# Attention heads paired for all four 64x64 tiles of the array, a state update in column halves, and a state without zero blocks

## The chip, the cores and the metric

The kernel runs on one core of a Trainium2 chip (trn2). Times are device microseconds of one execution. The time before is 762.54 us (median of six executions, 761.15 to 762.91). When the prediction was made three of these were known, with a median of 762.65.

## The reference, cut to what matters

Attention with a decaying state (batch 4, 8 heads, 768 steps, head size 64), followed by a two-layer block on 3072 tokens (512 to 2048 to 512, float32 results):

```python
for t in range(S):
    state = gamma[None, :, None, None] * state + np.einsum('bhd,bhe->bhde', k[:, :, t], v[:, :, t])
    y[:, :, t] = scale * np.einsum('bhd,bhde->bhe', q[:, :, t], state)
...
h = x @ w_in
g = h * erf(np.maximum(h, 0.0) + np.log1p(np.exp(-np.abs(h))))
return g @ w_out
```

## The kernel before

The sequence is cut into 24 chunks of 128 steps (four sequences of six chunks; c is the position in the sequence). A chunk goes through these steps: T transposes queries and keys, S makes the scores (64-row tiles), M masks them on VectorE, O makes the outputs, U makes the state's increment, A adds it to the state. These steps are strewn between the products of the two-layer block, which TensorE does with a seven-product (Strassen-like) scheme after the first 512 tokens. Chunks 0 to 3 come first. Chunks 4 to 7 lie beside the first 512 tokens. Chunks 8 to 23 lie in the long stretch from 163 us.

```python
def load(j):
    ...
    for x, src in ((KQ[j][:, 0], k), (KQ[j][:, 1], q), (V[j], v)):
        nc.sync.dma_start(x, src[b, :, c * C : (c + 1) * C, :].rearrange("h p d -> p h d"))
...
state = const.tile([P, HP, P], F32, name="state")      # a pair of heads: two 64x64 blocks, the rest zeros
nc.gpsimd.memset(state, 0.0)
...
def ret_out(j):
    ...
    p = ret_psum()
    if c:
        for hp in range(HP):
            nc.tensor.matmul(
                p[:, hp, :], state[:, hp, :], QT[j][:, hp, :],
                start=(hp == 0), stop=False, skip_group_check=True,
            )
    for hp in range(HP):
        for s in range(2):
            nc.tensor.matmul(
                p[s * D : (s + 1) * D, hp, :], V[j][:, 2 * hp + s, :], AM[j][:, s, hp, :],
                start=(not c and hp == 0), stop=True, skip_group_check=True,
            )
    nc.scalar.copy(XC[m][:, :, i * C : (i + 1) * C], p)

def ret_state(j):
    ...
        for hp in range(HP):
            nc.tensor.matmul(
                p[:, hp, :],
                KQ[j][:, 0, 2 * hp : 2 * hp + 2, :].rearrange("p h d -> p (h d)"),
                V[j][:, 2 * hp : 2 * hp + 2, :].rearrange("p h d -> p (h d)"),
                start=True, stop=True,
            )

def ret_add(j):
    for s in range(2):
        own = slice(s * D, (s + 1) * D)
        ... # state[own, :, own] += SU[j][own, :, own], or a copy at c == 0
```

The weights arrive as float64 and are converted on VectorE in small steps, which `pace(n)` deals out beside the other work. The last of them are the sums for the split products.

Of the kernel before, what the change touches and what calls it, by code (L numbers as in the profile page):

```python
# [12 lines left out]
F32 = mybir.dt.float32  # L13
# [3 lines left out]
ALU = mybir.AluOpType  # L17
PSUM = bass.MemoryType.PSUM

P = 128  # L20
C = 128
TCH = 512
FG = 4
SCH = 256
CV = 2



IN = {"11": 0, "12": 1, "21": 2, "22": 3, "S3": 2, "S1": 4, "S2": 5, "S4": 6}
# [12 lines left out]
def kernel(  # L42
# [13 lines left out]
    nc = tc.nc  # L56
    B, H, S, D = q.shape
    d_model, d_ff = w_in.shape
    HP = H // 2
    NC = S // C  # L60
    NJ = B * NC
    n_k = d_model // P
    n_ft = d_ff // P
# [2 lines left out]
    N = FG * TCH  # L66
    DH = d_model // 2
    assert D == 64 and d_model == H * D and n_k == HP == 4 and S % C == 0 and NJ % JPC == 0
    assert n_ft == 4 * FG and SCH == 2 * C and TCH == 2 * SCH

    const = ctx.enter_context(tc.tile_pool(name="const", bufs=1))
    loads = ctx.enter_context(tc.tile_pool(name="loads", bufs=3))
# [8 lines left out]
    KQ, V = {}, {}  # L81

    def load(j):
        b, c = divmod(j, NC)
        KQ[j] = loads.tile([P, 2, H, D], F32, name="kq")
        V[j] = loads.tile([P, H, D], F32, name="v")
        for x, src in ((KQ[j][:, 0], k), (KQ[j][:, 1], q), (V[j], v)):
            nc.sync.dma_start(x, src[b, :, c * C : (c + 1) * C, :].rearrange("h p d -> p h d"))

    kq_s = const.tile([P, NC, 2, H], F32, name="kq_s")  # L90
    d_s = const.tile([P, 2, HP], F32, name="d_s")

    w_in_sb = const.tile([P, 2, 7, 2, FG * P], F32, name="w_in_sb")
# [27 lines left out]
    place = [n % 4 if n < n_p - 4 else (n - n_p + 4) % 3 for n in range(n_p)]  # L121

    def load_piece(n):
        which, i = pieces[n]
        w = raws[place[n]]
        if which == "in":
            nc.sync.dma_start(
                w.rearrange("p (g f) -> p g f", g=n_k),
                w_in[:, i * 2 * P : (i + 1) * 2 * P].rearrange("(g p) f -> p g f", p=P),
            )  # L130
        else:
            for d in range(2):
                nc.sync.dma_start(
                    w.rearrange("p (d f c) -> p d f c", d=2, f=2)[:, d],
                    w_out[i * 2 * P : (i + 1) * 2 * P, d * DH : (d + 1) * DH].rearrange(
                        "(f p) c -> p f c", p=P
                    ),
                )
# [99 lines left out]
    def pace(n):  # L238

        nonlocal room  # L240
        room += n
        while room >= 1:
            next(weight_steps, None)
            room -= 1
# [5 lines left out]
            room -= 1  # L250

    load_piece(0)
    nc.scalar.dma_start(kq_s[:, 0, 0], decay_k)
    for s in range(2):
        nc.scalar.dma_start(d_s[:, s], decay_s[s * D : s * D + 1, :].to_broadcast([P, HP]))
    load(0)
    load_piece(1)
    load(1)
    load_piece(2)
    load(2)  # L260
    load_piece(3)

# [6 lines left out]
        out=causal, in_=causal, compare_op=ALU.is_ge, fill=0.0,  # L269
        base=0, pattern=[[1, C]], channel_multiplier=-1,  # L270
    )

    state = const.tile([P, HP, P], F32, name="state")
    nc.gpsimd.memset(state, 0.0)


    unscale = 1.0 / math.sqrt(D)
# [1 line left out]
    def query_scale(c):  # L279
        nc.vector.reciprocal(kq_s[:, c, 1], kq_s[:, c, 0])  # L280
        nc.vector.tensor_scalar(kq_s[:, c, 1], kq_s[:, c, 1], unscale, None, op0=ALU.mult)

    query_scale(0)

    def other_scales():
        back = const.tile([P, 2, HP], F32, name="back")
        nc.vector.reciprocal(back, d_s)
        for c in range(1, NC):
            by_head = [kq_s[:, i, 0].rearrange("p (h s) -> p s h", s=2) for i in (c, c - 1)]
            nc.gpsimd.tensor_tensor(by_head[0], by_head[1], back, op=ALU.mult)  # L290
        query_scale(slice(1, NC))


    QT, KT, SC, AM, XC, SU = {}, {}, {}, {}, {}, {}
# [4 lines left out]
    def ret_psum():  # L299

        pool = next(psum_turn) if early else ps_r
        return pool.tile([P, HP, C], F32, name="hp" if pool is ps_h else "r")
# [14 lines left out]
    def ret_transpose(j):  # L317
        assert j in scaled
        for i, (name, store) in enumerate((("k", KT), ("q", QT))):
            p = ret_psum()  # L320
            for hp in range(HP):
                nc.tensor.transpose(  # L322
                    p[:, hp, :],
                    KQ[j][:, i, 2 * hp : 2 * hp + 2, :].rearrange("p h d -> p (h d)"),
                    ident,
                )
            store[j] = ret.tile([P, HP, C], F32, name=name + "T")
            nc.scalar.copy(store[j], p)
        pace(1)
# [22 lines left out]
    def ret_out(j):  # L352
        c = j % NC
        m, i = divmod(j, JPC)
        if i == 0:
            XC[m] = ret.tile([P, HP, TCH], F32, name="xT")
        p = ret_psum()


        if c:  # L360
            for hp in range(HP):
                nc.tensor.matmul(  # L362
                    p[:, hp, :], state[:, hp, :], QT[j][:, hp, :],
                    start=(hp == 0), stop=False, skip_group_check=True,
                )
        for hp in range(HP):
            for s in range(2):
                nc.tensor.matmul(  # L368
                    p[s * D : (s + 1) * D, hp, :], V[j][:, 2 * hp + s, :], AM[j][:, s, hp, :],
                    start=(not c and hp == 0), stop=True, skip_group_check=True,  # L370
                )
        nc.scalar.copy(XC[m][:, :, i * C : (i + 1) * C], p)  # L372
        pace(1.7)

    def ret_state(j):
        c = j % NC
        if c < NC - 1:
            p = SU[j] = ret_psum()
            for hp in range(HP):
                nc.tensor.matmul(  # L380
                    p[:, hp, :],
                    KQ[j][:, 0, 2 * hp : 2 * hp + 2, :].rearrange("p h d -> p (h d)"),
                    V[j][:, 2 * hp : 2 * hp + 2, :].rearrange("p h d -> p (h d)"),
                    start=True,
                    stop=True,
                )
            pace(1)
        if j + 3 < NJ:
            load(j + 3)

    def ret_add(j):
        if j not in SU:
            return
        for s in range(2):
            own = slice(s * D, (s + 1) * D)
            if j % NC:
                nc.vector.tensor_tensor(
                    state[own, :, own], state[own, :, own], SU[j][own, :, own], op=ALU.add
                )
            else:  # L400
                nc.vector.tensor_copy(state[own, :, own], SU[j][own, :, own])
        pace(-0.8)


    HS, E, O = {}, {}, {}
# [76 lines left out]
    def chunk_of(g):  # L482
        return TCH // SCH + (g - G0) // 2
# [100 lines left out]
    def put_part(m, step):  # L584
# [26 lines left out]

    K_, T, S_, M, O_, U, A = (
        ret_scale, ret_transpose, ret_scores, ret_mask, ret_out, ret_state, ret_add
    )


    for f, *args in (
        (pace, 3), (K_, 0), (T, 0), (pace, 3.1), (S_, 0), (M, 0), (other_scales,), (K_, 1),
        (O_, 0), (T, 1), (U, 0), (pace, 1.5), (A, 0), (S_, 1), (M, 1), (K_, 2),
        (O_, 1), (T, 2), (U, 1), (pace, 1.5), (A, 1), (S_, 2), (M, 2), (K_, 3),  # L620
        (O_, 2), (T, 3), (U, 2), (pace, 0.5), (A, 2), (S_, 3), (pace, 0.5), (M, 3), (K_, 4),
        (O_, 3), (U, 3),
    ):
        f(*args)
# [29 lines left out]
    j = 2 * JPC  # L654
# [51 lines left out]
    g, m = NG - 1, chunk_of(NG - 1)  # L706
# [47 lines left out]
```

## Time and profile before

| | before |
|---|---|
| time, median of six | 762.54 us |
| TensorE busy | 731.1 us, 96% |
| 0 to 53 us | VectorE 41.6 of 53 us busy, DMA engines 0.92 to 0.99 |

The table by stage and its reading stand in the prediction.

```profile
PE hp L513 <- issue: 3.7, 1, 3.7
```

The columns are the waiter, what ended the wait, us in total, how often, and the longest. On the profile page below, "issue" is time in which the profile shows no cause.

### The profile page before, as it was taken

The numbers are of one execution on the slowest core, as the hardware profiler recorded it, in microseconds if no ns is written. First come the engines' busy times: TensorE is split into PE (matmuls) and PEld (weight loads), VectorE is DVE, ScalarE is ACT, GpSimd is POOL, SyncE is SP. The second block draws the span as 40 slices with busy tenths as digits, with TensorE's granted clock in tenths as the row PEclk, the third lists the DMA queues.
The fourth block names the chain that finished last, engine by engine and source line by source line (L and its number), as shares of the span: only waits on it lengthen the run. The fifth ranks groups of instructions, "written<-read, shape, count | busy, mean of one in ns | idle before, by whom it ended". The sixth has DMA issues, their size and how long they took to land.

```text
span 760.7 us, 11046 instructions
## 1 busy us (share of the span) xinstructions
PE 731.1 (96%) x4896; PEld 622.6 (82%) x4896; DVE 361.4 (48%) x482; ACT 272.4 (36%) x295; POOL 31.7 (4%) x29
## 2 busy tenths in 40 slices
PE   3889999989999999999999999999999999999996
PEld 2755445448699999999999999999999999999995
DVE  5897899994324334333253153163163152153323
ACT  1334636231533423414424424424234144324430
POOL 1000001000010110010010110100000000000000
PEclk9999999998999999999999999999999999999999
DMA  9977544102120120220220220220200000000000
GB/s 230 273 182 186 153 141 123 56 0 42 56 42 9 35 70 2 41 70 2 42 71 1 42 70 1 42 62 9 43 29 1 1 28 1 1 28 1 1 28 28
DMA packets 87391, 42.66 MB, mean 56 GB/s; under 512 B 76080, under 2 KB 76080, under 8 KB 87344
## 3 DMA queue, kind: packets, MB, share of 16 engines
q1 hardware_dynamic: 86912, 41.95, 21.4%
q8 instruction: 38, 0.62, 0.4%
q14 instruction: 9, 0.07, 0.0%
q10 hardware_dynamic: 432, 0.01, 0.0%
HBM read 35.66 MB, written 6.29 MB: 55 GB/s over the span
## 4 chain that ended last, share of the span: by engine, by line
PE 90%; DVE 5%; ACT 3%; issue 2%; DMA 1%; DVEq 0%; ACTq 0%
PE hp L513 33%; PE o L570 30%; PE o L456 7%; PE hp L443 6%; PE r L335 3%; PE r L368 3%; PE r L322 2%; PE r L362 2%; PE r L380 2%; DMA w_out_sb<-in_moe_w_in_dram 1%; ACT e L412 1%; DVE am L347 1%; DVE kq L313 1%; ACT e L413 1%; ACT L412 1%
## 5 line engine op out<-in xcount | busy, mean ns | idle before, releaser
L513 PE MATMUL hp<-xs,w_in_sb 128*128 128x128 f32 x1280 | 160.6, 280 | 3.9 <-issue 3.7
L513 PEld LDWEIGHTS hp<-xs,w_in_sb 128*128 128x128 f32 x1280 | 152.0, 193 | 10.8 <-issue 7.1
L570 PE MATMUL o<-w_out_sb,h 128*128 128x256 f32 x640 | 141.6, 379 | 0.0
L432 DVE TENSOR_TENSOR e<-h,e 128x1024 f32<-128x1024 f32 x44 | 51.9, 1221 | 182.7 <-ACT e L413 182.7
L570 PEld LDWEIGHTS o<-w_out_sb,h 128*128 128x128 f32 x640 | 121.6, 190 | 16.5
L513 PE MATMUL hp<-xT,w_in_sb 128*128 128x128 f32 x960 | 113.7, 275 | 0.0
L513 PEld LDWEIGHTS hp<-xT,w_in_sb 128*128 128x128 f32 x960 | 111.9, 192 | 1.9 <-issue 1.0
L570 PE MATMUL o<-w_out_sb,e 128*128 128x256 f32 x480 | 110.3, 379 | 0.9 <-DVE e L432 0.9
L570 PEld LDWEIGHTS o<-w_out_sb,e 128*128 128x128 f32 x480 | 88.2, 190 | 11.7 <-DVE e L432 1.3
L412 ACT ACT_TABLE_LOAD x24 | 30.8, 1283 | 91.4 <-PE o L570 89.4
L443 PE MATMUL hp<-xT,w_in_sb 128*128 128x512 f32 x128 | 58.9, 608 | 0.0
L538 DVE TENSOR_TENSOR h<-h,hp 128x512 f32<-128x512 f32 x20 | 13.7, 687 | 83.3 <-PE hp L513 83.3
L533 DVE TENSOR_TENSOR h<-h,hp 128x512 f32<-128x512 f32 x20 | 13.8, 688 | 80.7 <-ACT h L531 80.7
L313 POOL TENSOR_TENSOR kq<-kq,kq_s 128x1024 f32<-128x1024 f32 x15 | 29.1, 1940 | 498.3 <-DMA kq<-in_q_dram 476.8
L443 PEld LDWEIGHTS hp<-xT,w_in_sb 128*128 128x128 f32 x128 | 24.0, 194 | 27.0 <-issue 26.7
L372 ACT COPY xT<-r 128x512 f32<-128x512 f32 x24 | 14.0, 585 | 88.9 <-PE r L368 88.9
L412 ACT ACTIVATE e<-h 128x2048 f32<-128x2048 f32 x22 | 42.0, 1911 | 0.2
L413 ACT ACTIVATE e<-e 128x2048 f32<-128x2048 f32 x22 | 42.0, 1910 | 0.2
L347 DVE TENSOR_TENSOR am<-r,causal 128x512 f32<-128x512 f32 x44 | 28.5, 684 | 21.4 <-PE r L335 20.8
L322 PE MATMUL r<-ident,kq 128*128 128x128 f32 x176 | 24.8, 284 | 14.0 <-DVE kq L313 10.8
L536 ACT COPY h<-hp 128x512 f32<-128x512 f32 x20 | 11.7, 585 | 71.9 <-PE hp L513 71.9
L322 PEld LDWEIGHTS r<-ident,kq 128*128 128x128 f32 x176 | 21.0, 147 | 15.9 <-issue 12.1
(84 smaller groups left out, 694.1 us busy)
## 6 DMA issues: line engine op xcount, KB each, us to landing
w_out_sb<-in_moe_w_out_dram SPq DMA_DIRECT2D x14, 512.0 KB, 5.1
kq<-in_k_dram SPq DMA_DIRECT2D x24, 256.0 KB, 3.5
kq<-in_q_dram SPq DMA_DIRECT2D x24, 256.0 KB, 4.2
v<-in_v_dram SPq DMA_DIRECT2D x24, 256.0 KB, 4.5
w_in_sb<-in_moe_w_in_dram SPq DMA_DIRECT2D x6, 1024.0 KB, 5.5
out_dram<-r SPq DMA_DIRECT2D x24, 256.0 KB, 2.3
w_out_sb<-in_moe_w_in_dram SPq DMA_DIRECT2D x2, 1024.0 KB, 6.9
w_in_sb<-in_moe_w_out_dram SPq DMA_DIRECT2D x2, 512.0 KB, 3.9
```

The source lines that it names most:

```text
L313: engine.tensor_tensor(KQ[j], KQ[j], by, op=ALU.mult)
L322: nc.tensor.transpose(p[:, hp, :], KQ[j][:, i, 2 * hp : 2 * hp + 2, :].rearrange("p h d -> p (h d)"), ident,)
L335: nc.tensor.matmul(pp[s][:, hp, :], KT[j][s * D : (s + 1) * D, hp, :], QT[j][s * D : (s + 1) * D, hp, :], start=True, stop=True,)
L347: nc.vector.tensor_tensor(AM[j][:, s], SC[j][s], causal[:, None, :].to_broadcast([P, HP, C]), op=ALU.mult)
L368: nc.tensor.matmul(p[s * D : (s + 1) * D, hp, :], V[j][:, 2 * hp + s, :], AM[j][:, s, hp, :], start=(not c and hp == 0), stop=True, skip_g ...
L412: nc.scalar.activation(E[g], HS[g], AF.Softplus)
L413: nc.scalar.activation(E[g], E[g], AF.Erf)
L432: nc.vector.tensor_tensor(E[g][:, half], HS[g][:, half], E[g][:, half], op=ALU.mult)
L443: nc.tensor.matmul(p, w_in_of(ft, kk), XC[0][:, kk, :], start=(kk == 0), stop=(kk == n_k - 1))
L456: nc.tensor.matmul(O[0][tt].rearrange("p (d c) -> p d c", d=2), E[g][:, u * TCH + tt * P : u * TCH + (tt + 1) * P], w_out_of(ft), start=(f ...
L513: nc.tensor.matmul(bank[:, u, :], w_in_sb[:, s, IN[a], kk, u * P : (u + 1) * P], XS[m][b][:, kk, :], start=(p in (1, 2, 5) and u == 0 and ...
L570: nc.tensor.matmul(O[m][i][:, half, :], G[g][a][:, u * P : (u + 1) * P], w_out_sb[:, s, OUT[b], u, :], start=i not in started, stop=(s == ...
```

## The change

The intent is to do the two products that waste half of the array at half the work. The state loses its zero blocks. Each head's query-state product takes a 64x64 tile, and heads are paired so that successive products fall on all four. The state update makes only the diagonal blocks, two at a time in the halves of the columns. For this the heads of k and q are loaded in the order 0, 3, 1, 2, 4, 7, 5, 6, so that the two heads of a pair lie side by side for the transposes. This splits their transfers.

```diff
+PAIRS = ((0, 3), (1, 2), (4, 7), (5, 6))
+MOVES = ((0, 0), (3, 1), (1, 2), (2, 3))
 def load(j):
-        for x, src in ((KQ[j][:, 0], k), (KQ[j][:, 1], q), (V[j], v)):
-            nc.sync.dma_start(x, src[b, :, c * C : (c + 1) * C, :].rearrange("h p d -> p h d"))
+        for i, src in enumerate((k, q)):
+            for of, to in MOVES:
+                nc.sync.dma_start(
+                    KQ[j][:, i].rearrange("p (a b) d -> p a b d", a=2)[:, :, to],
+                    src[b, :, now, :].rearrange("(a b) p d -> p a b d", a=2)[:, :, of],
+                )
+        nc.sync.dma_start(V[j], v[b, :, now, :].rearrange("h p d -> p h d"))
 ... (the decay factors are put into the same order by eight tiny copies on VectorE)
-    state = const.tile([P, HP, P], F32, name="state")
-    nc.gpsimd.memset(state, 0.0)
+    state = const.tile([P, HP, D], F32, name="state")
 def ret_out(j):
-        p = ret_psum()
+        pp = [ret_psum() for _ in range(2)]
+        def place(h, r):
+            return pp[r][h % 2 * D : (h % 2 + 1) * D, h // 4, :]
         if c:
-            for hp in range(HP):
-                nc.tensor.matmul(p[:, hp, :], state[:, hp, :], QT[j][:, hp, :], ...)
+            for u, pair in enumerate(PAIRS):
+                for r, h in enumerate(pair):
+                    own = slice(r * D, (r + 1) * D)
+                    nc.tensor.matmul(place(h, r), state[own, u, :], QT[j][own, u, :], ...)
 ... (the value products go to the same places)
-        nc.scalar.copy(XC[m][:, :, i * C : (i + 1) * C], p)
-        pace(1.7)
+        for r in range(2):
+            nc.scalar.copy(XC[m][:, r::2, i * C : (i + 1) * C], pp[r][:, :2, :])
+        pace(1.5)
 def ret_state(j):
+            for u, pair in enumerate(PAIRS):
+                for r, h in enumerate(pair):
+                    nc.tensor.matmul(
+                        p[r * D : (r + 1) * D, u, :D], KQ[j][:, 0, 2 * u + r, :], V[j][:, h, :],
+                        start=True, stop=True,
+                    )
 def ret_add(j):
+        new = SU[j][:, :, :D]        # one instruction on 128 partitions instead of two on 64
-        pace(-0.8)
+        pace(-0.4)
```

More of the change, by code (lines that the diff above doesn't have):

```diff
@@ L68 @@
     assert D == 64 and d_model == H * D and n_k == HP == 4 and S % C == 0 and NJ % JPC == 0
-    assert n_ft == 4 * FG and SCH == 2 * C and TCH == 2 * SCH
+    assert H == 8 and n_ft == 4 * FG and SCH == 2 * C and TCH == 2 * SCH
     const = ctx.enter_context(tc.tile_pool(name="const", bufs=1))
@@ L86, in load @@
         V[j] = loads.tile([P, H, D], F32, name="v")
-        for x, src in ((KQ[j][:, 0], k), (KQ[j][:, 1], q), (V[j], v)):
-            nc.sync.dma_start(x, src[b, :, c * C : (c + 1) * C, :].rearrange("h p d -> p h d"))
+        now = slice(c * C, (c + 1) * C)
+        for i, src in enumerate((k, q)):
[5 more added lines that the diff above has]
+        nc.sync.dma_start(V[j], v[b, :, now, :].rearrange("h p d -> p h d"))
     kq_s = const.tile([P, NC, 2, H], F32, name="kq_s")
+    d_k = const.tile([P, H], F32, name="d_k")
     d_s = const.tile([P, 2, HP], F32, name="d_s")
@@ L252 @@
     load_piece(0)
-    nc.scalar.dma_start(kq_s[:, 0, 0], decay_k)
+    nc.scalar.dma_start(d_k, decay_k)
     for s in range(2):
@@ L281, in query_scale, with in_pairs @@
         nc.vector.tensor_scalar(kq_s[:, c, 1], kq_s[:, c, 1], unscale, None, op0=ALU.mult)
+    def in_pairs(to, of):
+        for a, b in MOVES:
+            nc.vector.tensor_copy(
+                to.rearrange("p (a b) -> p a b", a=2)[:, :, b],
+                of.rearrange("p (a b) -> p a b", a=2)[:, :, a],
+            )
+    in_pairs(kq_s[:, 0, 0], d_k)
     query_scale(0)
     def other_scales():
-        back = const.tile([P, 2, HP], F32, name="back")
-        nc.vector.reciprocal(back, d_s)
+        back, by = (const.tile([P, H], F32, name=name) for name in ("back", "by"))
+        nc.vector.reciprocal(back, d_s.rearrange("p s h -> p h s"))
+        in_pairs(by, back)
         for c in range(1, NC):
-            by_head = [kq_s[:, i, 0].rearrange("p (h s) -> p s h", s=2) for i in (c, c - 1)]
-            nc.gpsimd.tensor_tensor(by_head[0], by_head[1], back, op=ALU.mult)
+            nc.gpsimd.tensor_tensor(kq_s[:, c, 0], kq_s[:, c - 1, 0], by, op=ALU.mult)
         query_scale(slice(1, NC))
@@ L320, in ret_transpose @@
             p = ret_psum()
-            for hp in range(HP):
+            for u in range(HP):
                 nc.tensor.transpose(
-                    p[:, hp, :],
-                    KQ[j][:, i, 2 * hp : 2 * hp + 2, :].rearrange("p h d -> p (h d)"),
+                    p[:, u, :],
+                    KQ[j][:, i, 2 * u : 2 * u + 2, :].rearrange("p h d -> p (h d)"),
                     ident,
@@ L356, in ret_out @@
             XC[m] = ret.tile([P, HP, TCH], F32, name="xT")
-        p = ret_psum()
+        pp = [ret_psum() for _ in range(2)]
+        def place(h, r):
+            return pp[r][h % 2 * D : (h % 2 + 1) * D, h // 4, :]
         if c:
-            for hp in range(HP):
-                nc.tensor.matmul(
-                    p[:, hp, :], state[:, hp, :], QT[j][:, hp, :],
-                    start=(hp == 0), stop=False, skip_group_check=True,
-                )
-        for hp in range(HP):
-            for s in range(2):
-                nc.tensor.matmul(
-                    p[s * D : (s + 1) * D, hp, :], V[j][:, 2 * hp + s, :], AM[j][:, s, hp, :],
-                    start=(not c and hp == 0), stop=True, skip_group_check=True,
-                )
-        nc.scalar.copy(XC[m][:, :, i * C : (i + 1) * C], p)
-        pace(1.7)
+            for u, pair in enumerate(PAIRS):
+                for r, h in enumerate(pair):
+                    own = slice(r * D, (r + 1) * D)
+                    nc.tensor.matmul(
+                        place(h, r), state[own, u, :], QT[j][own, u, :],
+                        start=(h < 4), stop=False, skip_group_check=True,
+                    )
+        for h in range(H):
+            u, r = next((u, pair.index(h)) for u, pair in enumerate(PAIRS) if h in pair)
+            nc.tensor.matmul(
+                place(h, r), V[j][:, h, :], AM[j][:, r, u, :],
+                start=(not c and h < 4), stop=True, skip_group_check=True,
+            )
+        for r in range(2):
+            nc.scalar.copy(XC[m][:, r::2, i * C : (i + 1) * C], pp[r][:, :2, :])
+        pace(1.5)
     def ret_state(j):
@@ L378, in ret_state @@
             p = SU[j] = ret_psum()
-            for hp in range(HP):
-                nc.tensor.matmul(
-                    p[:, hp, :],
-                    KQ[j][:, 0, 2 * hp : 2 * hp + 2, :].rearrange("p h d -> p (h d)"),
-                    V[j][:, 2 * hp : 2 * hp + 2, :].rearrange("p h d -> p (h d)"),
-                    start=True,
-                    stop=True,
-                )
+            for u, pair in enumerate(PAIRS):
+                for r, h in enumerate(pair):
+                    nc.tensor.matmul(
+                        p[r * D : (r + 1) * D, u, :D], KQ[j][:, 0, 2 * u + r, :], V[j][:, h, :],
+                        start=True, stop=True,
+                    )
             pace(1)
@@ L393, in ret_add @@
             return
-        for s in range(2):
-            own = slice(s * D, (s + 1) * D)
-            if j % NC:
-                nc.vector.tensor_tensor(
-                    state[own, :, own], state[own, :, own], SU[j][own, :, own], op=ALU.add
-                )
-            else:
-                nc.vector.tensor_copy(state[own, :, own], SU[j][own, :, own])
-        pace(-0.8)
+        new = SU[j][:, :, :D]
+        if j % NC:
+            nc.vector.tensor_tensor(state, state, new, op=ALU.add)
+        else:
+            nc.vector.tensor_copy(state, new)
+        pace(-0.4)
     HS, E, O = {}, {}, {}
```

## The prediction

> **What bounds the kernel now.** I read four views in this order: the busy summary, the busy table by stretch, the matmul timeline of one chunk, and the chain of work that ended last. First the summary:
>
> ```profile
> PE 731.1 (96%) x4896; PEld 622.6 (82%) x4896; DVE 361.4 (48%) x482; ACT 272.4 (36%) x295; POOL 31.7 (4%) x29
> ```
>
> TensorE is busy for 96% of the span. That average hides two regimes, so I cut the span by stage:
>
> ```profile
> core 0: us, PE busy (x) PEld busy (x) DVE busy (x) ACT busy (x) POOL busy (x), PEclk, DMA share, GB/s
> 20.00:53.00 33.00, 28.21 (x216) 21.38 (x216) 30.16 (x38) 10.35 (x16) 0.00 (x0) 1.00 0.99 247
> 53.00:84.00 31.00, 29.23 (x146) 16.91 (x148) 24.90 (x29) 15.08 (x18) 0.00 (x0) 0.94 0.56 153
> 84.00:163.00 79.00, 79.00 (x248) 37.89 (x247) 76.97 (x74) 36.96 (x35) 4.38 (x2) 1.00 0.35 100
> 163.00:662.00 499.00, 495.31 (x3663) 456.04 (x3662) 183.69 (x280) 172.91 (x192) 24.72 (x13) 0.99 0.13 31
> ```
>
> From 163 us on, TensorE alone is the bound, and 16 of the 24 chunks of attention (numbers 8 to 23) run there. Before 53 us VectorE (30.2 of 33) and the DMA engines (share 0.99) are both nearly full, and TensorE is the follower. What a TensorE saving is worth is therefore read in the long stretch. One chunk of it, matmuls only:
>
> ```profile
> 441.00 1.04 PE L322 MATMUL r<-ident,kq 128*128 128x128 f32 x8
> 441.88 1.95 PE L513 MATMUL hp<-xs,w_in_sb 128*128 128x128 f32 x16
> 443.76 1.16 PE L335 MATMUL r<-qT,kT 64*128 64x128 f32 x16
> 444.85 2.05 PE L513 MATMUL hp<-xs,w_in_sb 128*128 128x128 f32 x16
> 446.74 1.06 PE L362 MATMUL r<-qT,state 128*128 128x128 f32 x8
> 447.73 1.09 PE L368 MATMUL r<-am,v 128*64 128x128 f32 x16
> ```
>
> The first column is the start. Differences of starts are what a block costs, because ends are modelled and overlap the next block. Each float32 product of the program is two records, so x8 is four products. L322 takes 441.88 - 441.00 = 0.88 for 8 records. In longer runs the rate is 3.57 us for 32 records, 0.1116 each. I call that one step.
>
> The two half-size blocks are the lesson. L335 (row halves) and L368 (column halves) have 16 records each, but last 1.09 and 1.02, not 16 x 0.1116 = 1.79. Two tiles run side by side, so each block is 8 steps = 0.893 plus 0.20 or 0.13. The extra is the price of changing the array's shape. L513 before L335 lasts 1.88 where 16 steps are 1.786, so 0.094 is lost at the change. L513 after L335 lasts 1.89, so 0.10 is lost at its beginning. L362 ahead of L368 lasts 0.99 where 8 steps are 0.893, again 0.094 at the change.
>
> So a change of shape costs 0.094 us to drain plus the first weight load, which is not hidden: about 0.10 us for 128 columns and about 0.045 for 64 (1.02 - 0.893 - 0.094 = 0.04). Weight loads support the ratio:
>
> ```profile
> L335 PEld LDWEIGHTS r<-qT,kT 64*128 64x128 f32 x352 | 25.1, 196 | 7.4 <-ACT qT L328 2.6 <-issue 2.5
> L368 PEld LDWEIGHTS r<-am,v 128*64 128x64 f32 x384 | 22.0, 140 | 6.9 <-DVE am L347 3.8 <-issue 0.8
> ```
>
> Half the columns save 56 ns, so a 64-column load occupies some 0.05 us.
>
> The chain of work that ended last puts what the change touches at 2.0% (L362) and 1.9% (L380) of the span:
>
> ```profile
> by line: PE hp L513 33.4%; PE o L570 30.0%; PE o L456 7.2%; PE hp L443 5.7%; PE r L335 3.2%; PE r L368 3.2%; PE r L322 2.4%; PE r L362 2.0%; PE r L380 1.9%; issue 1.6%; DMA w_out_sb<-in_moe_w_in_dram 0.8%; ACT e L412 0.8%; DVE am L347 0.6%;
> ```
>
> That is 30 us in all. Halving both at no cost would give 15 us, 2.0% of 762.65. This caps what TensorE can yield before the changes of shape are paid.
>
> **What the Trainium skill says.** "TensorEngine Tiling (Array Packing)", Key Properties, says that changing the tiling mode drains TensorE while changing only the tile does not. The trace agrees: 0.094 us at each change. "TensorE: Matmul & The Clock Gate", Part 3, says that a pack of tiles takes about one matmul and 4 ns per further tile, sixteen tiles included. For two tiles the trace agrees (16 records in about 8 steps); no run here has shown four. The same page, Part 1, gives a floor of about 25 ns between starts of matmuls. With four tiles the wanted spacing is 0.1116/4 = 28 ns, and with two tiles of 64 columns it is 30 ns. Both are barely above that floor, and the densest block in this trace has 56 ns. "DMA: Bandwidth & Descriptors", Rules for kernel authors, warns that transfers under 64 KB are mostly overhead. The loads of k and q go from 256 KB to exactly 64 KB each.
>
> **The change, part by part.**
>
> 1. *Query times state.* Four products with a 128x128 stationary operand, half of it zeros, become eight of 64x64 that can fill all four quadrants. 16 records in groups of four are 4 steps = 0.446 instead of 0.893: minus 0.447 us per chunk that has a state.
>
> 2. *State update.* Four 128x128 products, half of whose output is thrown away, become eight with 64 stationary columns and 64 moving columns, two side by side: 8 steps of a shorter kind. From 128, 256 and 512 moving columns (0.1116, 0.216, 0.429 us between starts) a column costs 0.00081 us, so 64 columns take 0.1116 - 0.052 = 0.060 us (estimate), just longer than the 0.05 us weight load beneath it. 8 x 0.060 = 0.48 instead of 0.893: minus 0.413 us.
>
> 3. *Changes of shape.* Query-state was of full shape like its neighbour; now its entry costs 0.094 + 0.045 = 0.139 more. Its exit to the value product was a change already. The state update stood between full-shape work; now it costs 0.139 to enter and 0.194 to leave. In sum plus 0.472 us per chunk, more than half of what parts 1 and 2 give.
>
> Chunks 8 to 23 hold 11 of positions 1 to 4 in their sequence (both parts): -0.447 - 0.413 + 0.472 = -0.388 each. Three stand at position 5 (no update): -0.447 + 0.139 = -0.308. Two stand at position 0 (no query-state): -0.413 + 0.333 = -0.080. The sum is 4.27 + 0.92 + 0.16 = 5.4 us, on the path because TensorE there never waits.
>
> Chunks 4 to 7 run at 59 to 122 us, mostly TensorE-bound. In chunk 4 the state update directly follows the value product in the same 128x64 shape, so it saves more, about 0.9; one score block also waits 0.6 us there for the state addition, which becomes shorter. With 0.3, 0.1 and 0.4 for the other three: about 2 us.
>
> 4. *VectorE.* The state addition was two instructions of about 0.42 us on 64 partitions; it becomes one of 128x256, and 128x256 float32 instructions of the same engine also take 0.42. Three such pairs lie on the early chain (30.83, 36.9, 42.11 us), and the copy at 23.80: about 1.5 us gained if VectorE holds there. Eight tiny copies come in for the head order: four while VectorE waits for the first weights anyway, four ahead of the scales, which chunk 1 waits for: 4 x 0.17 (the 128x8 instruction takes 171 ns) = about 0.6 us lost.
>
> 5. *ScalarE.* One eviction of 128x512 (0.585) becomes two of 128x256 (0.378 each), +0.17 us. The next user of those banks comes 16 records, 1.8 us, later: hidden.
>
> 6. *Loads.* Three transfers per chunk become nine, the same bytes and the same 256-byte rows. An issue occupies SyncE's queue for 0.37 us at least, so the query tile of chunk 0 is fully issued some 2 us later, but the 1 MB weight piece ahead of it keeps the engines busy until 6.7 us, and VectorE comes to it at 9.4 only. I allow +0.5 to +1 us before 53 us and nothing later, where loads run three chunks ahead.
>
> 7. *Order of conversion steps.* The pacing numbers shift by +0.2 step per chunk: within noise.
>
> Sum: -5.4 - 2.0 - 1.5 + 0.6 + 0.7 = -7.6 us, so 755.0 us.
>
> **Rivals.**
>
> *Four tiles don't run four at once.* If only two quadrants stream together, query-state takes 8 steps as before and the changes of shape remain: 18 chunk positions x 0.447 = 8 us come back and the time is about 763. For it: no block in this trace runs four tiles. Against: row halves and column halves each overlap nearly perfectly, and each row half writes its own bank.
>
> *The state update is bound by issue or weight loads, not by 64 columns.* If a pair still takes a full step of 0.11, the gain of 0.413 vanishes for 20 chunks and 0.333 is paid: about 762. For it: 4 instructions every 60 ns is twice the densest rate seen. Against: the weight load alone takes 0.05.
>
> *The early stretch gets worse.* Before 53 us the DMA engines are 99% busy; if 48 more transfers each cost them something, 1 to 3 us are added, and the saving of VectorE is lost: about 757 to 758.
>
> *A new wait for the masks.* Query-state now writes two banks, those of the scores, so it needs both masks. Where the second mask ends 446.41 and query-state starts 446.74, there is 0.33 us to spare, 0.33 to 0.50 in all later chunks: no wait expected.
>
> **Range and chances.** The middle case is 755.0. If all overlaps and the early part goes well, 752. If one of the first two rivals holds, 761 to 763. I hold each of those two at 15 to 20%, so the upper end gets more room: 751.5 to 761.5. The 2% marks are 747.4 and 777.9. The first is almost the cap of free halving, which the changes of shape forbid; the second would need several us of new waits.
>
> **What would show each step.** In the timeline after: starts of the query-state block and of the value block about 0.58 us apart (4 steps, 0.045, 0.094; 1.02 or more refutes four at once); the state update block about 0.62 (8 x 0.060 + 0.045 + 0.094); the block ahead of each longer by 0.094. The long stretch from the first split product to the last should be 5 to 6 us shorter. If chunk spacing there shrinks by less than 0.2 us per chunk, the tile arithmetic is wrong; if it shrinks by 0.39 and the total still doesn't, the early stretch is at fault.

## More of the kernel before

The long stretch, one group of products after the other:

```python
for g in range(G0, NG):
    if first:
        x_sums(g)          # input sums for the split products, on VectorE
        gated(g - 1)
    hidden_part(g, 1)
    hidden_part(g, 2)
    ...  T(j);  hidden_part(g, 6);  S_(j); M(j);  hidden_part(g, 5);  O_(j);  hidden_part(g, 7);  U(j); A(j)
    ...  project_part(g - 1, 1);  hidden_part(g, 4);  hidden_part(g, 3);  more project_part
```

## The result, and the profile after

The changed kernel takes 755.27 us (median of six, 754.19 to 758.39), and the kernel before 762.54. The ratio is 0.9916 (95% interval 0.9895 to 0.9936), inside the 2% band. All outputs are right.

First, the matmul timeline of the same chunk as in the prediction (number 17, position 5), from the block ahead of query-state on:

```profile
440.21 2.05 PE L534 MATMUL hp<-xs,w_in_sb 128*128 128x128 f32 x16
442.19 0.67 PE L387 MATMUL r<-qT,state 64*64 64x128 f32 x16
442.79 1.09 PE L393 MATMUL r<-am,v 128*64 128x128 f32 x16
```

The query-state block (L387) lasts 442.79 - 442.19 = 0.60 us with 16 records; before it lasted 0.99 with 8. The block ahead of it (L534) lasts 1.98 instead of 1.89, which is the drain of 0.09 that now precedes the change of shape. Position 5 has no state update, so here is that of chunk 16 (position 4), in the same view, before:

```profile
420.88 1.06 PE L380 MATMUL r<-v,kq 128*128 128x128 f32 x8
421.77 1.89 PE L570 MATMUL o<-w_out_sb,e 128*128 128x256 f32 x8
```

and after:

```profile
416.41 0.69 PE L407 MATMUL r<-v,kq 128*64 128x64 f32 x16
417.03 1.99 PE L591 MATMUL o<-w_out_sb,e 128*128 128x256 f32 x8
418.86 0.38 PE L534 MATMUL hp<-xs,w_in_sb 128*128 128x128 f32 x2
```

It lasts 0.62 instead of 0.89, and L591 after it lasts 1.83 where before it was 1.73 (421.77 to 423.50). I read the 0.10 as the weight load of the first record of the next shape, which nothing hides.

Second, the table of stages. The columns are busy time per engine, then the granted clock of TensorE, the DMA share and GB/s:

```profile
0.00:20.00 20.00, 6.17 (x40) 4.80 (x40) 10.75 (x22) 4.33 (x6) 2.17 (x13) 1.00 0.81 220
20.00:53.00 33.00, 27.50 (x272) 19.73 (x272) 27.84 (x34) 10.63 (x19) 0.00 (x0) 0.95 0.81 216
```

Before 53 us the DMA engines are less busy than before (0.81, where it was 0.92 and 0.99). They are starved, not overloaded. SyncE's queue shows why (start, duration of all issues, transfers):

```profile
0.80 0.43 SPq L139 DMA_DIRECT2D w_out_sb<-in_moe_w_in_dram  x1
1.30 2.30 SPq L95 DMA_DIRECT2D kq<-in_k_dram  x4
4.71 3.37 SPq L95 DMA_DIRECT2D kq<-in_q_dram  x4
```

The queries of chunk 0 are issued by 8.1 us; before, it was 2.4.

Third, the chain of work that ended last, between 163 and 176 us. In this view the columns are start, length and what. The kernel before:

```profile
168.11 0.50 ACT qT L328
168.61 3.01 issue
171.62 3.76 PE hp L513 x16
```

and the changed one:

```profile
168.56 0.50 ACT qT L346
169.06 1.87 issue
170.93 3.59 PE hp L534 x16
```

TensorE arrives later than before (169.06 against 168.61) and still goes on earlier (170.93 against 171.62). So something other than TensorE decides when the long stretch begins.

Where the 7.40 us between the two profiled spans (760.74 and 753.34) lie follows from starts in these timelines:

| stretch | gain, us | how it is worked out |
|---|---|---|
| to the first split product with summed inputs | 0.69 | 171.62 - 170.93 |
| from there to the transposes of chunk 9, less chunk 8's share | 0.92 | (204.72 - 171.62) - (202.73 - 170.93) - 0.38 |
| chunks 8 to 23 | 5.21 | 11 x 0.378 + 3 x 0.296 + 2 x 0.082, from block lengths |
| the tail after chunk 23 | 0.58 | the rest |

The second row shows the clock, but only in the kernel before. After its 3.7 us of standing still TensorE ran at half clock there, and for a shorter time in the changed kernel (the 0.50 and 0.72 stand in the column before the DMA share). The kernel before first, then the changed one:

```profile
172.00:176.00 4.00, 4.00 (x22) 3.78 (x23) 3.97 (x5) 0.59 (x1) 0.00 (x0) 0.50 0.01 4
```

```profile
172.00:176.00 4.00, 4.00 (x33) 3.74 (x33) 3.86 (x5) 0.59 (x1) 0.00 (x0) 0.72 0.00 0
```

What ends this stretch is the start of the second split product with summed inputs. In the kernel before it starts 5.54 us after the first (177.16), although VectorE's addition ahead of it had ended at 175.18 (174.49 + 0.69), so there the half clock cost up to 1.9 us. In the changed kernel it starts 4.62 us after the first (175.55), just when that addition ends (174.82 + 0.68 = 175.50). So here VectorE set it, not the clock: e8 and e7, with the clock at 1.00, take 4.63 and 4.75 us for the same stretch, and their profiles name this addition as what the product waits for. The difference, 5.54 - 4.62, is the 0.92. These are the additions, before and after:

```profile
174.49 0.69 DVE L526 TENSOR_TENSOR h<-h,hp 128x512 f32<-128x512 f32 x1
```

```profile
174.82 0.68 DVE L547 TENSOR_TENSOR h<-h,hp 128x512 f32<-128x512 f32 x1
```

Half of the last row has a cause in the trace. In the kernel before one split product near the end waits for VectorE; in the changed kernel none does there, and the distance between the two kernels' starts grows by 0.29 us at this place (6.83 to 7.12). The other 0.29 lies behind the last product, and its cause is open.

```profile
673.59 1.60 PE L513 MATMUL hp<-xs,w_in_sb 128*128 128x128 f32 x12 [0.21 <-DVE h L526]
```

### The profile page after: what moved, and what is told of

Its sections match the earlier page's. It is cut to its first block, busy times and chain, and to the rows that moved or that the text cites. A ratio compares the mean times of both kernels' runs of the same rounds, so it can differ in the third digit from the quotient of the medians. Undisturbed runs are those within 1.5% of the kernel's fastest.

```text
span 753.3 us, 11963 instructions
## 1 busy us (share of the span) xinstructions
PE 720.7 (96%) x5216; PEld 605.7 (80%) x5216; DVE 353.3 (47%) x470; ACT 274.0 (36%) x319; POOL 31.4 (4%) x28
## 4 chain that ended last, share of the span: by engine, by line
PE 91%; DVE 2%; ACT 2%; DMA 2%; issue 1%; SPq 0%; ACTq 0%; DVEq 0%
PE hp L534 34%; PE o L591 32%; PE o L477 7%; PE hp L464 6%; PE r L353 3%; PE r L393 3%; PE r L340 2%; PE r L407 1%; PE r L387 1%; DMA d_s<-decay_s_dram 1%; DVE am L365 1%; ACT e L434 1%; ACT e L433 1%; DVE kq L331 0%; SPq L95 0%
## 5 line engine op out<-in xcount | busy, mean ns | idle before, releaser
L534 PE MATMUL hp<-xs,w_in_sb 128*128 128x128 f32 x1280 | 160.3, 280 | 2.6 <-issue 2.6
L534 PEld LDWEIGHTS hp<-xs,w_in_sb 128*128 128x128 f32 x1280 | 151.9, 193 | 9.4 <-issue 6.0
L591 PE MATMUL o<-w_out_sb,h 128*128 128x256 f32 x640 | 141.6, 379 | 0.0
L591 PEld LDWEIGHTS o<-w_out_sb,h 128*128 128x128 f32 x640 | 121.6, 190 | 16.5
L534 PE MATMUL hp<-xT,w_in_sb 128*128 128x128 f32 x960 | 113.7, 275 | 0.0
L534 PEld LDWEIGHTS hp<-xT,w_in_sb 128*128 128x128 f32 x960 | 111.9, 192 | 1.9 <-issue 1.0
L591 PE MATMUL o<-w_out_sb,e 128*128 128x256 f32 x480 | 111.5, 382 | 0.9 <-DVE e L453 0.9
L591 PEld LDWEIGHTS o<-w_out_sb,e 128*128 128x128 f32 x480 | 88.1, 190 | 12.5 <-DVE e L453 1.3
L398 ACT COPY xT<-r 128x256 f32<-128x256 f32 x44 | 14.5, 377 | 71.9 <-PE r L393 71.9
```

The lines of the kernel that those rows point to most:

```text
L534: nc.tensor.matmul(bank[:, u, :], w_in_sb[:, s, IN[a], kk, u * P : (u + 1) * P], XS[m][b][:, kk, :], start=(p in (1, 2, 5) and u == 0 and ...
L591: nc.tensor.matmul(O[m][i][:, half, :], G[g][a][:, u * P : (u + 1) * P], w_out_sb[:, s, OUT[b], u, :], start=i not in started, stop=(s == ...
```

## The experiments

The theory is that the tile arithmetic of the prediction holds in the long stretch, and that before 171 us other engines decide. The rivals are that the four tiles or the update's shape gain something else than worked out, that the loads are hidden, or that TensorE decides throughout. All runs were timed over five rounds beside the kernel before. "Goes on" is the start of the first split product with summed inputs. "Spacing" is the time between the transposes of chunks 16 and 17 (position 4), from the matmul timeline of the profiled execution.

| run | median, us | ratio to before (95%) | goes on, us | spacing, us |
|---|---|---|---|---|
| before | 762.54 | | 171.62 | 29.76 |
| changed | 755.27 | 0.9916 (0.9895 to 0.9936) | 170.93 | 29.38 |
| changed, again | 754.33 | 0.9895 (0.9877 to 0.9912) | 171.14 | 29.38 |
| e2, loads split in the kernel before | 764.23 | 1.0038 (1.0019 to 1.0058) | 174.17 | 29.76 |
| e3, two quadrants | 761.79 | 0.9999 (0.9982 to 1.0015) | 172.63 | 29.80 |
| e4, update halves alone | 760.93 | 0.9985 (0.9963 to 1.0006) | 168.46 | 29.68 |
| e7, state added in two halves | 758.50 | 0.9961 (0.9943 to 0.9980) | 173.06 | 29.38 |
| e1, rows of w_in reordered instead | 764.19 | 1.0026 (1.0011 to 1.0041) | 179.84 | 29.38 |
| e5, update joined to the value product | 750.10 | 0.9845 (0.9825 to 0.9865) | 170.94 | 29.03 |
| e6, e1 and e5 | 759.19 | 0.9963 (0.9948 to 0.9978) | 179.72 | 29.03 |
| e8, head h with h+4 | 752.66 | 0.9874 (0.9852 to 0.9895) | 168.62 | 29.38 |
| e11, weight sums held back | 750.51 | 0.9846 (0.9829 to 0.9863) | 169.10 | 29.38 |
| e9, e8 and e5 | 747.32 | 0.9806 (0.9789 to 0.9824) | 167.51 | 29.03 |
| e10, e8, e5 and e11 | 743.45 | 0.9751 (0.9733 to 0.9770) | 165.39 | 29.03 |

The spacing repeats to 0.01 us. What comes before 171 us varies by some microseconds from execution to execution (single executions of the kernel before lay between 759.7 and 764.1), so "goes on" of a single profile is read with that in mind: e4 changes little there and still goes on 3.2 us earlier than the kernel before.

### e2: the loads split, alone

```diff
-        for x, src in ((KQ[j][:, 0], k), (KQ[j][:, 1], q), (V[j], v)):
-            nc.sync.dma_start(x, src[b, :, c * C : (c + 1) * C, :].rearrange("h p d -> p h d"))
+        for i, src in enumerate((k, q)):
+            for t in range(4):
+                nc.sync.dma_start(
+                    KQ[j][:, i].rearrange("p (a b) d -> p a b d", a=2)[:, :, t],
+                    src[b, :, now, :].rearrange("(a b) p d -> p a b d", a=2)[:, :, t])
+        nc.sync.dma_start(V[j], v[b, :, now, :].rearrange("h p d -> p h d"))
```

> The kernel before, with only the loads changed: k and q of a chunk come in four transfers each (two heads, 64 KB) into their old places. If the split loads are what the early stretch lost (theory): first query-key transposes at about 11.5 instead of 10.8 us, later arrival of chunks 1 to 5, total +1 to +3 us (763.5 to 765.5) and more spread between executions. If the loads are hidden (rival): 762.5 within 0.5 us. In both, chunk spacing after 171 us stays 29.76 us.

The run took 764.23 us against 762.18 for the kernel before, a ratio of 1.0038, so the loads are not hidden. Kernels are compared only within the same rounds. The first transposes start at 11.26 us (10.77 before). The table of stages shows the same starving as in the changed kernel: a share of 0.82 and 0.86 of the DMA engines, where it was 0.92 and 0.99.

```profile
0.00:20.00 20.00, 6.58 (x40) 5.21 (x40) 10.64 (x16) 4.19 (x5) 2.63 (x14) 1.00 0.82 228
20.00:53.00 33.00, 29.43 (x216) 22.47 (x216) 29.62 (x37) 10.34 (x16) 0.00 (x0) 1.00 0.86 222
```

### e3: two quadrants instead of four

```diff
-PAIRS = ((0, 3), (1, 2), (4, 7), (5, 6))
+PAIRS = ((0, 1), (2, 3), (4, 5), (6, 7))
-            return pp[r][h % 2 * D : (h % 2 + 1) * D, h // 4, :]
+            return pp[r][r * D : (r + 1) * D, h // 2, :]
```

(The loads and the decay factors are those of the kernel before; the two evictions take 64 partitions each.)

> The changed kernel with neighbouring heads paired as before (no reordering, plain loads), so that the 64x64 query-state products lie on the two diagonal quadrants only. If four quadrants at once are what halves the block (theory): 8 steps, the query-state block grows from 0.598 to about 1.03 us, chunk spacing at positions 1 to 4 from 29.38 to about 29.82, and the total is 760 to 762, worse than the changed kernel by 6 to 7 us less what the plain loads give back (1 to 3 us). If the block is bound by something else, such as issue (rival): the block stays near 0.6 and the total is 753 to 755.

```profile
447.29 1.09 PE L372 MATMUL r<-qT,state 64*64 64x128 f32 x16
448.31 1.09 PE L378 MATMUL r<-am,v 128*64 128x128 f32 x16
449.33 0.94 PE L520 MATMUL hp<-xs,w_in_sb 128*128 128x128 f32 x6
```

The block lasts 1.02 us where four quadrants need 0.60: the same 16 products of the same size, only elsewhere in the array. Spacing is 29.80, a little worse than before the change, and the time is that of the kernel before. The pairing is the whole gain of the query-state part. Small tiles without it save no step and still pay for the change of shape. Although its loads are the plain ones, this run goes on at 172.63, later than the changed kernel, so it doesn't show the loads giving anything back.

### e4: the state update in column halves, alone

```diff
             for hp in range(HP):
-                nc.tensor.matmul(p[:, hp, :], KQ[...2 * hp : 2 * hp + 2...], V[...2 * hp : 2 * hp + 2...], ...)
+                for s in range(2):
+                    own = slice(s * D, (s + 1) * D)
+                    nc.tensor.matmul(p[own, hp, own], KQ[j][:, 0, 2 * hp + s, :], V[j][:, 2 * hp + s, :], ...)
```

> The kernel before with only the state update in column halves (eight 128x64 products of 64 columns, written to the same diagonal blocks). Theory: the block goes from 0.893 to about 0.62 us, but entering costs 0.14 and leaving 0.10 more, so a chunk gains 0.08 us: spacing 29.68 instead of 29.76, total 761 to 762. Rival (halving the work halves the time): 0.4 us per chunk, 20 chunks, total about 754.5.

```profile
415.35 2.05 PE L512 MATMUL hp<-xs,w_in_sb 128*128 128x128 f32 x16
417.33 0.69 PE L382 MATMUL r<-v,kq 128*64 128x64 f32 x16
417.94 1.99 PE L569 MATMUL o<-w_out_sb,e 128*128 128x256 f32 x8
419.77 0.49 PE L512 MATMUL hp<-xs,w_in_sb 128*128 128x128 f32 x3
```

The block shrinks by 0.28 us (0.894 to 0.615). The block before it grows by 0.094 (1.888 to 1.982) and the block after it by 0.102 (1.729 to 1.831), so 0.08 remains. Spacing says the same: 29.68 instead of 29.76. Thirteen such chunks are 1.1 us of the long stretch. The total, 760.93 with 758.3 to 762.9 in single executions, cannot be told from no change by its interval; the spacing can.

### e7: the state added in two halves again

```diff
+        for s in range(2):
+            own = slice(s * D, (s + 1) * D)
             if j % NC:
-                nc.vector.tensor_tensor(state, state, new, op=ALU.add)
+                nc.vector.tensor_tensor(state[own], state[own], new[own], op=ALU.add)
```

> The changed kernel with the state addition (and first copy) done in two instructions of 64 partitions, as before. Theory: VectorE's queue, not TensorE, decides when the first split product of the long stretch can go on at 170.9 us, so 0.42 us more per chunk for eight chunks moves that moment by 1 to 3.4 us, and the total is 756 to 759. Rival (TensorE's savings set that moment; VectorE is slack): 170.9 within 0.3 us and the total 755 to 756. Chunk spacing after it stays 29.38 us either way.

The run took 758.50 us, with a ratio of 0.9961 where the changed kernel has 0.9916 and 0.9895. TensorE goes on at 173.06, 1.9 us later than in the repeat of the changed kernel. A little more VectorE work, and nothing else, costs 3.2 us by the median and 4.2 by the repeat's (the two profiled executions differ by 2.0). In its profile the clock from 172 to 176 us was 1.00, so the clock's fall after the wait is not the same in every execution.

### e11: the weight sums held back

```diff
     def pace(n):
+        if hold and ("sums in", 1) in done:
+            return
...
         hidden_part(g, 1)
         hidden_part(g, 2)
+        hold = False
```

> The changed kernel with VectorE's last eight weight sums (not needed before about 200 us) held back until the first split products have started, so that they don't stand ahead of the input sums that TensorE waits for at 171 us. Theory (the order in VectorE's queue sets that moment and the wait lowers the clock for some microseconds after it): the wait of 2.6 us goes, TensorE goes on at about 168.4, and the clock from 172 to 176 stays near 1.0, some 0.7 us more; total 3 to 3.5 us below the changed kernel, about 751.5. Rival (TensorE only meets the next wait, for the gate or the sums, later): total within 1 us of the changed kernel.

The chain of the changed kernel's repeat, from 163 us on. Here the profile names the cause that it called "issue" in the first profile:

```profile
163.22 4.64 DVE w_out_sb L214 x4
167.86 0.02 issue
167.88 2.36 DVE w_out_sb L214 x2
170.24 0.35 DVE xs L517
```

and, after two more input sums, up to the second split product:

```profile
171.71 2.27 DVE r L453 x2
173.98 1.14 DVE w_out_sb L214
175.11 0.61 DVE h L547
175.72 0.04 issue
175.77 0.45 PE hp L534
```

and with the sums held back:

```profile
164.82 3.57 PE hp L537 x32
168.39 0.87 PE r L343 x8
169.27 1.79 PE hp L537 x16
171.05 1.09 PE r L356 x16
```

Before, seven sums of output weights that nobody needs yet stand in VectorE's queue ahead of the input sums (xs) that TensorE waits for, and an eighth ahead of the addition (h) that the second split product waits for. In this run two of the eight are issued before the hold takes effect, and six wait. The chain is then TensorE from end to end, and the clock from 172 to 176 us is 1.00. The time is 750.51 us against 754.33. Of the 3.8 us, 2.0 are the earlier start (171.14 to 169.10). The transposes of chunk 9 come 3.77 us earlier (203.03 to 199.26), so 1.7 more are gained just behind that. The clock was 0.57 there in the repeat, but the chain shows VectorE as what TensorE waited for: the second split product came 4.63 us after the first in the repeat, as in e8 at full clock, and comes 2.97 us after it here (172.07). So the part of the theory that puts 0.7 us down to the clock is not shown. The run does show that VectorE's order, not TensorE, set the beginning of the long stretch.

### The changed kernel again, and e5: the update joined to the value product

> The changed kernel itself, for comparison on the same chip: 755.3 us, as the six executions on record, with single executions up to 758.

It came at 754.33 us (753.64 to 755.35); the first six lay between 754.19 and 758.39. For e5, for chunks from 8 on:

```diff
+        join = j >= 2 * JPC and c < NC - 1
+        if join:                       # directly after the value products, in the free half of their second bank
+            new = pp[1][:, 2:, :].rearrange("p a (b d) -> p (a b) d", d=D)
+            for u, pair in enumerate(PAIRS):
+                for r, h in enumerate(pair):
+                    nc.tensor.matmul(new[r * D : (r + 1) * D, u, :], KQ[j][:, 0, 2 * u + r, :], V[j][:, h, :], ...)
+            ... # VectorE adds new to the state, then evicts pp[1]; ScalarE evicts pp[0] alone
```

> The changed kernel with the state update of chunks 8 to 23 issued directly after the value product, which has the same 128x64 shape, into the free half of that product's second bank; VectorE then adds the state and evicts that bank. Theory: two changes of shape go (0.094 + 0.045 and 0.094 + 0.10 = 0.333 us) for 13 chunks: spacing 29.05 instead of 29.38, 4.3 us in all, total about 751. Rival: a change of shape is not what the block costs, or a new wait for the evictions takes its place: spacing 29.3 or more, total 754 to 757.

```profile
410.42 0.67 PE L390 MATMUL r<-qT,state 64*64 64x128 f32 x16
411.02 1.09 PE L396 MATMUL r<-am,v 128*64 128x128 f32 x16
411.94 0.64 PE L405 MATMUL r<-v,kq 128*64 128x64 f32 x16
412.51 2.05 PE L554 MATMUL hp<-xs,w_in_sb 128*128 128x128 f32 x16
```

Value product and update together last 412.51 - 411.02 = 1.49 us. Apart they last 1.02 + 0.62 and cost 0.20 more in their neighbours. Spacing falls to 29.03, so 0.35 per chunk; the time is 750.10 us against 754.33. The price of a change of shape, which the prediction read from the trace, is thus shown by removing two of them.

### e1 and e6: another way to plain loads, which failed

```diff
 def load_piece(n):            # a 1 MB piece of w_in, its rows in the order of the new places of the heads
-            nc.sync.dma_start(w.rearrange("p (g f) -> p g f", g=n_k), w_in[...].rearrange("(g p) f -> p g f", p=P))
+            for s in range(2):
+                for r in range(2):
+                    nc.sync.dma_start(
+                        w[s * D : (s + 1) * D].rearrange("p (a r f) -> p a r f", a=2, r=2)[:, :, r],
+                        w_in[...].rearrange("(a e p) f -> p a e f", e=4, p=D)[:, :, 2 * (s ^ r) + r])
```

> The changed kernel with plain loads of k and q: neighbours stay paired, the four-quadrant placement permutes the features of the attention output instead, and the rows of w_in are loaded in that order (8 weight pieces in four transfers of 256 KB each; no tiny copies). Theory: what the split loads and tiny copies cost before 60 us (about 1.7 us on the kernel before) comes back, long stretch unchanged at spacing 29.38: 753 to 754.5. Rival: the early stretch is held by VectorE and not by the loads, total as the changed kernel within 0.7 us.

> Both edits at once. If they act on different stretches (theory), their gains add: about 749.5 us, 1.7% below the kernel before. If both only move the moment that VectorE sets at 171 us (rival), the gain is that of the joined update alone, 751.

Neither expectation came true. e1 is 764.19 us: the long stretch is as expected (29.38), but it begins 8.7 us later than in the repeat. The view of DMA issues (transfers, KB each, median us to landing) shows the cause:

```profile
w_in_sb<-in_moe_w_in_dram SPq DMA_DIRECT2D x24, 256.0 KB, 6.0
w_out_sb<-in_moe_w_in_dram SPq DMA_DIRECT2D x8, 256.0 KB, 5.9
```

A quarter of a piece to 64 partitions lands as late as a whole piece to 128 did (5.5 and 6.9 us before). The engines were full (share 1.01 in the first 20 us) at 177 GB/s, where the kernel before moved 237. That agrees with the Trainium skill, "DMA: Bandwidth & Descriptors", Rules for kernel authors, which advises against two transfers to disjoint partition halves. So e1 answers another question. It does show that a delay of the loads reaches the end undiminished. e6 lies 5.0 us below e1, the gain of the joined update again.

### e8: head h with head h+4

```diff
-PAIRS = ((0, 3), (1, 2), (4, 7), (5, 6))
+PAIRS = ((0, 4), (1, 5), (2, 6), (3, 7))
...
-            for of, to in MOVES: ...                    # four transfers of two heads
+            for r in range(2):
+                nc.sync.dma_start(
+                    KQ[j][:, i].rearrange("p (u r) d -> p u r d", r=2)[:, :, r],
+                    src[b, 4 * r : 4 * r + 4, now, :].rearrange("u p d -> p u d"))
-            return pp[r][h % 2 * D : (h % 2 + 1) * D, h // 4, :]
+            return pp[r][h % 2 * D : (h % 2 + 1) * D, h % 4 // 2, :]
```

> The changed kernel with head h paired with head h+4. All four quadrants are still used in turn, but the order of heads is now regular, so k and q come in two transfers of 128 KB each instead of four of 64 KB, and each tiny copy is one instruction instead of four. Theory (the split loads and tiny copies cost about 1.7 us of the early stretch): half of it back, 0.7 to 1.5 us below the changed kernel, first split product at 169.5 to 170.3 instead of 171.0 us. Rival (VectorE's queue alone sets that moment): within 0.5 us of the changed kernel.

The run took 752.66 us, 1.7 below the repeat; TensorE goes on at 168.62, 2.5 us earlier. That is more than expected. The DMA share in the first two stages is back at 0.97 and 0.93, and VectorE's chain at 161 to 171 us is the same but earlier. I read this as the loads limiting how early VectorE gets its work, while VectorE decides when TensorE goes on. The run changes the loads and the tiny copies together, so their shares are not separated; no run changes the copies alone.

### e9 and e10: the parts together

> Heads paired with h+4 and the state update joined to the value product. If the early stretch and the long stretch add (theory): the 4.5 us of the joined update and 0.7 to 1.5 us more: 748.5 to 749.5. If the pairing gives nothing (rival): 750.1.

> Pairing with h+4, joined update, sums held back. If all three add: about 745.5 to 746.5, over 2% below the kernel before. If the held-back sums only move the wait elsewhere: 748.5 to 749.5.

e9 took 747.32 us, 1.2 below the lower end of what was expected. e10 took 743.45 us (742.11 to 743.94), 2.5% below the kernel before and better than both kernels. Alone, e8, e5 and e11 gain 1.7, 4.2 and 3.8 us on the repeat of the changed kernel, 9.7 together; all three at once gain 10.9. So they add, with 1.2 us more that no run explains; 1.1 of it is there already in e9 (7.0, where e8 and e5 alone give 5.9).

## Why the prediction was right

**The number.** Predicted 755.0, range 751.5 to 761.5, measured 755.27, inside the range.

**Parts 1 to 3, the tile arithmetic: right in each step.** Query-state block 0.58 predicted, 0.60 measured. Update block 0.62 predicted, 0.615 measured. Per chunk -0.388, -0.308 and -0.080 predicted, -0.378, -0.296 and -0.082 measured. Sum 5.4 predicted, 5.2 measured; the transposes of chunks 9 to 22 alone draw together by 4.16 us, as the block lengths say. e3 shows that four quadrants at once are the cause. e4 shows that the update pays for its change of shape almost all that it gains. e5 shows the price of the change itself. One support was weak: the weight-load records of the transposes (L322), with all 128 columns, last 147 ns too, so the 56 ns between L335 and L368 are not shown to come from the columns. A small slip is in the first rival, which counts 18 chunks with a state; there are 20, of which 14 lie in the long stretch.

**Chunks 4 to 7, "about 2 us": wrong in kind.** TensorE does catch up there: it comes to the transposes of chunk 5 3.08 us later than before (56.58 against 53.50), and to those of chunk 8 only 0.45 later (167.34 against 166.89). How much of that is the tiles is open, since the clock from 53 to 84 us was 0.94 before and 1.00 after. But from 169 us TensorE waits for VectorE's input sums, so what it gains earlier does not set the time. I had read TensorE as the bound because it is busy 79.00 of 79 us; VectorE, at 76.97, had the queue that ended later. e7 and e11 show it. In this stretch there were also waits that I had not foreseen: in chunk 4 the update now waits 0.25 us for an eviction, because the outputs hold both banks, and a score block of chunk 6 waits 1.51 us for ScalarE's copy of the queries (0.65 before; not tested).

**Part 4, VectorE: right in direction, and worth more than I said.** e7, which takes the shorter addition away again, costs 3 to 4 us. The 0.6 us for the tiny copies was not tested alone.

**Part 6, the loads: mis-sized.** I allowed 0.5 to 1 us. In e2 they cost 2.0 us by the medians (764.23 against 762.18) and 2.9 by the ratio (0.0038 x 762). I had taken 0.37 us for an issue; the eight of chunk 0 took 0.58 (2.30/4) and 0.84 (3.37/4) each, so the queries were issued 5.7 us later and not 2, and VectorE waits 1.25 us for them. The mechanism was also not the one I feared: the engines were not overloaded but starved by the queue that issues nine transfers instead of three.

**Part 7, the order of the conversion steps: not noise.** The shifted pacing put one more weight sum ahead of the input sums, seven instead of six, and one ahead of the addition for the second split product. VectorE begins its last sums of the input weights 1.83 us earlier than before (157.09 against 158.92), but the input sums start only 0.69 earlier (169.95 against 170.64); the sum between takes 1.14. e11 moves these sums away, but no run restores the old order alone. Before and after:

```profile
163.58 7.14 DVE L202 TENSOR_TENSOR w_out_sb<-w_out_sb 128x1024 f32<-128x1024 f32 x6
```

```profile
161.75 8.28 DVE L214 TENSOR_TENSOR w_out_sb<-w_out_sb 128x1024 f32<-128x1024 f32 x7
```

**What came in their place.** All of part 4, part 6 and chunks 4 to 7 was -2.2 us in my sum. The profile has -0.69 to the point where TensorE goes on, -0.92 behind it, where the half clock cost only the kernel before, and -0.58 in the tail, together -2.19. The equality is luck. The second and third parts were in no step of mine.

**Rivals.** Four tiles not at once: refuted (0.60 us, and e3). Update bound by issue: refuted (pairs start 58 ns apart). Early stretch worse: true in its half about the loads, outweighed by VectorE. Mask wait: none seen in the long stretch.

## What to carry to other kernels

Count the changes of array shape before counting the work saved: here each cost 0.14 to 0.20 us, and putting two products of one shape side by side (e5) was worth four times the halving of one of them (e4: 0.08 us a chunk; e5: 0.35). Where two engines are both above 95% busy, look at which of their queues ends last at the next meeting point; a saving on the other is given back there. And when heads can be paired freely, choose the pairing that keeps the transfers large (e8), and let late-needed work wait behind what another engine needs next (e11).

## What the Trainium skill lacked or had wrong

- "TensorEngine Tiling (Array Packing)", Key Properties, says that a change of mode drains the array, but gives no size and doesn't say that the first weight load in the new mode is exposed. Here: 0.094 us plus 0.10 us for 128 columns or 0.05 us for 64, where the split into drain and weight load is my reading of the block lengths.
- "TensorE: Matmul & The Clock Gate", Part 1, has a floor of 25 ns between starts of matmuls. With four quadrants four matmuls start within 20 ns, 7 ns apart, and the next four 89 ns later: 27 ns on average. The floor did not hold between tiles; its Part 3 (about 4 ns per further tile) is the better guide, with 7 ns measured here. No run pushed the average below 25 ns.
- "DMA: Bandwidth & Descriptors", Rules for kernel authors, warns of small transfers as overhead. Here the cost lay on the issuing side: k and q of chunk 0 were issued by 8.1 us instead of 2.4, with the DMA engines' share falling from 0.99 to 0.81 in the next stage. Two transfers of 128 KB (e8) were enough to bring it back to 0.93.
- The half clock after TensorE stands still is on the page "TensorE: Matmul & The Clock Gate", Part 1. In these profiles the length of the wait alone did not decide it: it came after 3.69 us (the kernel before, 0.50 from 172 to 176 us) and after 2.55 and 2.43 (the changed kernel, 0.72 and 0.57), and not after 3.32 (e7) and 2.47 (e8). It cost the kernel before up to 1.9 us and the changed kernel nothing that the trace shows, because VectorE was later.
